# Where the four links of a weight scale's chain stand in a step of a fused attention and MLP kernel

## The chip, the cores and the metric

The kernel runs on one core of one Trainium2 chip. The metric is the device time of one execution in microseconds. The core has five engines with queues of their own: TensorE (PE; matmuls and, listed apart as PEld, weight loads), VectorE (DVE), ScalarE (ACT), GpSimd (POOL) and SyncE (SP, which here only issues transfers). An engine takes its instructions in the order in which the program lists them, and waits at each for the semaphores that it needs. So where an instruction stands in its engine's list decides what waits behind it. In order of time, three runs of the kernel before took 994.47, 989.99 and 993.67 us, with a median of 993.67.

## The reference

Causal attention over 4 batches of 8 heads, 576 positions and 64 dimensions, with an added bias from the running sum of `max(s, 0)`; then a first MLP, `relu(x w_in)^2 w_out`, and a second, `h cos(h) w_out` with `h = x w_in`, over 2304 tokens, model size 512 and hidden size 2048.

```python
scores = scale * np.matmul(q, k.transpose(0, 1, 3, 2))
cum = np.cumsum(np.maximum(s, 0.0), axis=-1)
bias = -(cum[:, :, :, None] - cum[:, :, None, :])
scores = np.where(causal, -1e9, scores + np.minimum(bias, 0.0))
x = softmax(scores) @ v            # then to (2304, 512)
h = np.maximum(x @ w_in, 0.0);  x = h * h @ w_out      # first MLP
h = x @ w2_in;  out = h * np.cos(h) @ w2_out           # second MLP
```

## The kernel before, in words

Products are made of parts: a weight tile is scaled by a power of two and split into a high half and the rest, and three products (high by high, high by low, low by high) stand for one.

The program's first part is a sequence of calls of `step()` (line 1236). I number them from 1. Call n emits the scores of attention job n - 1 (`emit_qk`), the mask and minimum of the job before (`emit_mask`, L593), the exponential (`emit_exp`, L616), the transposes of the probabilities (`emit_turn`, L629), their copy out of PSUM (L650), the products with V (`emit_pv`, L695), and every fourth call the transposes of an output (`turn`, L757), which ScalarE (`x_high`, L800) and VectorE (`x_low`, L816) read and split. A job is 128 queries of one head; the first sixteen heads have two jobs each, with 128 and 256 keys. From call 22 on a call also takes one or two slots of the first MLP: `g1` (L1078, twelve matmuls into `hps`), whose result ScalarE takes with Relu, square and cast (L1089 to L1091) and VectorE splits (L1097), and `g2` (L1107).

Beside that each call prepares weights of the first MLP, one half row of 512 columns at a time: loaded by SyncE (L207), rescaled by ScalarE (L924), put together from two integer halves by VectorE (L930, L934), then written as the high part by ScalarE (`w_hi`; L946 with a scale, L950 without) and the rest by VectorE (`w_lo`; L964, L969). `room()` and the buffers `st`, `xst` and four spare halves of `wt` say how many can be under way.

The high part of a `w_in` tile needs a scale, a power of two for each pair of tiles, and that has a chain of its own, which also serves two blocks of tokens (from V):

1. `gram()`: eight matmuls of the tiles with themselves (L831) into `xps[:, 384:512]`; the trace of this is the sum of the squares of each row's columns.
2. `gram_sums()`: VectorE multiplies with the identity and adds up along the row (L836).
3. `gram_total()`: a matmul with ones adds over the 128 rows (L845) into `xps[:, 264]`.
4. `gram_scale()`: VectorE takes the exponent (L853), POOL makes scale and inverse (L860, L866), and the pair goes on the list `wrest`, from which the next `w_step` takes it to `w_hi`.

The chain runs ten times: for eight pairs of tiles (pair 0 to 7) and for two blocks of tokens. Its PSUM tile `xps` is also that of the output's transposes (columns 0 to 255) and of V's sums (L459). In the kernel before, link 1 stands near the end of call n, link 2 at the head of call n + 1, link 3 behind the first MLP slot of that call, and link 4 ahead of the mask and of `w_step`, all in the same call. The trace of a pair stands in calls 8, 11, 14, 21, 24, 26, 29 and 32, that of the two blocks in calls 6 and 13. The list `later` holds work that is due at a given call; a call takes at most one entry from it.

Of the kernel before, what the change touches and what calls it, by code (L numbers as in the profile page):

```python
# [36 lines left out]
W_AHEAD = 2.5  # L37
GRAM, GSUM = 384, 264
SPARES = 4


def _weave(*chains):
# [81 lines left out]
V_STRIDE = 11  # L124
V_NEAR = 6
V_TIME = 7
X_AT = (4, 12)


@with_exitstack  # L130
def attention_moe_moe_kernel(
# [290 lines left out]
    def load_v(n):  # L422
        b, h, nch = heads[n][1], heads[n][2], (heads[n][7] + 127) // 128
        if n < EARLY:
            vd[n] = vown[n]
            return
        vb = at.tile([128, 5, 2, D], F16, tag="vb", bufs=4, name="vb")
        nc.sync.dma_start(out=vb[:, 0:nch], in_=v_d[b, h, :, 0:nch])
        vd[n] = vb
# [175 lines left out]
    def emit_exp(i):  # L605
        n, ti, q, r = jobs[i]
        h = heads[n][2]
        j = jd[i]
        x = h % 2
        if _paired(heads[n]):  # L610
            if x == 0:
                return
            r, x = 128, 0
        w, sb = j["w"], j["sb"]
        z = pd[n - h % 2]["z"]
        nc.scalar.activation(  # L616
            out=sb[0:r, 0:w], in_=sb[0:r, 0:w], func=ACTF.Exp, scale=-1.0, bias=j["nb"],
            accum_out=z[0:r, ti, x:x + 1],
        )
        if _paired(heads[n]):  # L620
            nc.scalar.copy(z[0:64, 0, 1:2], z[64:128, 0, 0:1])
# [11 lines left out]
    def p_turn():  # L633
        while turned:
            pt, p = turned.pop(0)
            nc.sync.dma_start_transpose(out=pt, in_=p)
# [147 lines left out]
    def x_high():  # L784
        for k, c, o, m, pt, _ in xcq:
            if k not in xb:
                xb[k] = (
                    m1.tile([128, KD, BT], F16, tag="xh", bufs=2, name="xh"),
                    m1.tile([128, KD, BT], F16, tag="xl", bufs=2, name="xl"),
                )  # L790
        while kept.get("go"):
            k = kept["go"].pop(0)
            for (o, m), cs in kept.pop(k).items():
                c0, c1 = min(cs), max(cs) + 1
                xs = [t[:, c0:c1, o:o + m] for t in (x32, *xb[k])]
                nc.scalar.activation(out=xs[1], in_=xs[0], func=ACTF.Copy, scale=xsc[:, k:k + 1])
                convq.append((k, xs))
        for k, c, o, m, pt, _ in xcq:
            if k in xready:
                nc.scalar.activation(  # L800
                    out=xb[k][0][:, c, o:o + m], in_=pt[:, 0:m], func=ACTF.Copy, scale=xsc[:, k:k + 1]
                )
            else:
                nc.scalar.copy(x32[:, c, o:o + m], pt[:, 0:m])
                kept.setdefault(k, {}).setdefault((o, m), []).append(c)
# [17 lines left out]
    def gram():  # L823

        if not gq or dq:
            return
        key, aps = gq.pop(0)
        out = xps[:, GRAM:GRAM + 128]
        for n, t in enumerate(aps):
            t = t.bitcast(BF16)[:, 1::2]  # L830
            nc.tensor.matmul(out, t, t, start=(n == 0), stop=(n == len(aps) - 1))  # L831
        dq.append(key)

    def gram_sums():
        for key in dq:
            nc.vector.scalar_tensor_tensor(  # L836
                out=gjunk, in0=xps[:, GRAM:GRAM + 128], scalar=1.0, in1=ident, op0=ALU.mult, op1=ALU.mult,
                accum_out=dss[:, key:key + 1],
            )
        oq.extend(dq)  # L840
        dq.clear()

    def gram_total():
        for key in oq:
            nc.tensor.matmul(xps[:, GSUM:GSUM + 1], ones, dss.bitcast(BF16)[:, 2 * key + 1:2 * key + 2])  # L845
        eq.extend(oq)
        oq.clear()

    def gram_scale():

        while eq:
            key = eq.pop(0)
            nc.vector.tensor_scalar(  # L853
                out=gex, in0=xps[:, GSUM:GSUM + 1].bitcast(I32), scalar1=24, scalar2=23, op0=ALU.logical_shift_right,
                op1=ALU.logical_shift_left,
            )
            sc, iv = (wsc1, wiv1) if key < NF // 2 else (xsc, xiv)
            c = key % (NF // 2)
            for t, a, b in ((sc, -1, 205), (iv, 1, 254 - 205)):
                nc.gpsimd.tensor_scalar(  # L860
                    out=t[:, c:c + 1].bitcast(I32), in0=gex, scalar1=a, scalar2=b << 23, op0=ALU.mult, op1=ALU.add
                )
            if sc is xsc:
                xready.add(c)
            else:
                nc.gpsimd.tensor_scalar(  # L866
                    out=hs1[:, 0, c:c + 1], in0=wiv1[:, c:c + 1], scalar1=xiv[:, 0:1], scalar2=1.0, op0=ALU.mult,
                    op1=ALU.mult,
                )
                wrest.extend(pairs.pop(c))  # L870
# [22 lines left out]
    def job(i):  # L893
        return jobs[i] if 0 <= i < NJ else None
# [16 lines left out]
    nw = [2, 0, 0]  # L911
# [27 lines left out]
    def w_hi(j):  # L939
        m, f, a = wq[j]  # L940
        if m == 0 and a == 0:
            t = wp.tile([128, 2, 512], F32, tag=f"w{2 * f}", name="wt")
            wt[0, f, 0] = t[:, 0].bitcast(F16).rearrange("p (a c) -> p a c", a=2)
            if f < SPARES:
                free.append(t[:, 1])
# [273 lines left out]
    def stage(s, i):  # L1219

        while stages[s] <= i and job(stages[s]):
            stages[s] += 1
            yield stages[s] - 1
# [7 lines left out]
    def values(i):  # L1231
        for j in stage(0, i - 2):
            if jobs[j][1] == 0:
                load_v(jobs[j][0])

    def step(moe=0, bits=0, attn=True):

        i = prog[0]
        held = len(xtq)
        prog[0] += attn  # L1240
        if attn:
            for j in stage(1, i - 2):
                emit_exp(j)
        x_high()
        if attn and job(i - 2):
            emit_turn(i - 2)
        if attn:
            heads_ahead(i, (next_, load_ext, 2))
        w_age()
        w_scales()  # L1250
        gram_sums()
        n = moe_slot() if moe else None
        gram_total()
        slow = bool(vq) and any(f is v_wait for f, g in vq[0])
        if slow:
            v_sums()
        if attn:
            heads_ahead(i, (nhigh, prep_high, 2))
        _weave(evacuate())
        y_evict()  # L1260
        if not attn or g2done[0] < 2:
            rests()
        if xcq and xcq[-1][-1] and xcq[-1][0] == 1:
            x_low()
        gram_scale()
        _weave(softmax_tail(i) if attn else None, w_step(bits), None if slow else v_early())
        x_low()
        rests()
        w_lows()
        if attn and job(i - 1) and jobs[i - 1][0] < EARLY:  # L1270
            for j in stage(1, i - 1):
                emit_exp(j)
        act(n)
        if attn:
            heads_ahead(i, (nlow, prep_low, 2))
        if slow:
            _weave(v_early())
        if not (attn and last_block(i)):
            y_store()
        if attn and job(i):  # L1280
            emit_qk(i)
        if attn and last_block(i):
            heads_ahead(i, (nraw, load_raw, 4))
        for _ in range(moe - 1):
            act(moe_slot())
            y_evict()
        w_sums()
        if attn:
            for j in stage(1, i - 1):
                emit_exp(j)  # L1290
        behind = any(job(j) and _paired(heads[jobs[j][0]]) for j in (i - 6, i - 5))
        if attn and not behind:
            values(i)
        turn(held if moe and i > last_job[0] + TURN_FROM else len(xtq))
        if not slow:
            v_sums()
        gram()
        if attn:
            for j in stage(3, i - LAG[0]):
                if j > i - lag(j):  # L1300
                    stages[3] -= 1
                    break
                emit_pv(j)
        if attn and behind:
            values(i)
        p_turn()
        w_ahead()
        if attn:
            heads_ahead(i, (nraw, load_raw, 4))
        v_late()  # L1310
        y_store()
        if later and prog[0] >= later[0][0]:
            later.pop(0)[1]()
# [18 lines left out]
    def w_age():  # L1332
        wsum.extend(wsq)
        wsq.clear()
# [18 lines left out]
    def w_lows():  # L1353
        while wlow:
            w_lo(wlow.pop(0))
# [71 lines left out]
    later.append((4, store_c1))  # L1427
    later.append((X_AT[0], lambda: early_scale(0)))
    later.append((6, lambda: v_own(1)))
    later.append((8, lambda: store_ones(nc.sync, EARLY, len(heads))))  # L1430
    later.append((11, store_c))
    later.append((X_AT[1], lambda: early_scale(1)))
    for n in seg0[EARLY // H:]:
# [280 lines left out]
```

## Time and profile before

| | |
|---|---|
| median of three runs | 993.67 us (989.99 to 994.47) |
| the profiled execution | 994.07 us, of which the span from first to last instruction is 992.2 us |
| mean granted TensorE clock | 0.973 of full speed |
| TensorE busy | 949.5 us, 96% of the span |
| VectorE busy | 724.9 us, 73% |
| ScalarE busy | 674.8 us, 68% |
| POOL busy | 171.9 us, 17% |

Shares over the whole span are means over unlike stages. The four links of the chain all fall in the first 110 us, and there the table has to be read stretch by stretch. In a list of instructions, what stands in brackets is the idle time of the engine just before, and what ended it. Matmuls are pipelined and the ends of their rows are modelled, so neighbouring rows overlap.

### The profile page before, as it was taken

To read this page: it belongs to the slowest core of one execution; us is meant where nothing else is said; L and a number is where in the kernel's file an instruction comes from. 1 tells how busy PE (TensorE), PEld (TensorE's weight loads), DVE (VectorE), ACT (ScalarE), POOL (GpSimd) and SP (SyncE) were. 2 spreads that over 40 slices of the span, in tenths; PEclk is the share of its full clock that TensorE was granted. 3 is DMA by queue.
4 is the path that set the end of the run, shared out by engine and by line. 5 is a ranking of instruction groups with operands and counts; after the bars stand their busy time and mean duration, and the time that the engine had idled before them with its cause. 6 is when DMAs were issued, how large, how long until landed. Compare 5 with 4: busy or idle time off the path is not lost.

```text
span 992.2 us, 20635 instructions
## 1 busy us (share of the span) xinstructions
PE 949.5 (96%) x7340; PEld 699.2 (70%) x7340; DVE 724.9 (73%) x1868; ACT 674.8 (68%) x1599; POOL 171.9 (17%) x279
## 2 busy tenths in 40 slices
PE   6888889999999999999999999999999999999998
PEld 5677778888899988889989987444544454444444
DVE  6758878777887877787898265798779865545555
ACT  6568877778888878778786587667657743334333
POOL 3001101111110111111111022431133340001101
PEclk8579899999999999999999999999999999999999
DMA  8766249865898986568899579210000000001001
GB/s 258 231 223 199 64 117 216 214 169 148 183 185 171 203 194 173 143 149 170 184 215 191 168 265 356 96 43 1 1 1 1 1 1 1 12 32 43 33 10 65
DMA packets 150520, 127.22 MB, mean 128 GB/s; under 512 B 107864, under 2 KB 125600, under 8 KB 150416
## 3 DMA queue, kind: packets, MB, share of 16 engines
q1 hardware_dynamic: 146512, 119.59, 46.8%
q0 software_dynamic: 3904, 6.30, 2.6%
q8 instruction: 58, 0.95, 0.4%
q14 instruction: 46, 0.38, 0.1%
HBM read 85.79 MB, written 15.83 MB: 102 GB/s over the span
## 4 chain that ended last, share of the span: by engine, by line
PE 76%; DVE 8%; ACT 7%; DMA 5%; issue 3%; SPq 1%; DVEq 0%; POOL 0%; ACTq 0%
PE hp L1535 19%; PE o L1590 18%; PE y L1107 15%; PE hps L1078 15%; PE qkp L575 4%; PE pvs L702 3%; DMA rw<-in_w_dram 2%; DMA raw<-in_qk_dram 2%; ACT sb L616 1%; ACT g L1089 1%; DVE k L418 1%; DVE sb L593 1%; ACT g L1090 1%; PE xps L757 1%; DMA early<-in_qk_dram 1%
## 5 line engine op out<-in xcount | busy, mean ns | idle before, releaser
L1107 PE MATMUL y<-gh,wt 128*128 128x256 f32 x1152 | 239.0, 290 | 2.1 <-DVE wt L969 2.1
L1078 PE MATMUL hps<-xh,wt 128*128 128x256 f16 x1152 | 217.0, 276 | 8.8 <-ACT g L1089 8.8
L1107 PEld LDWEIGHTS y<-gh,wt 128*128 128x128 f32 x1152 | 189.3, 191 | 3.8 <-DVE wt L969 2.6
L1078 PEld LDWEIGHTS <-wt 128*128 128x128 f16 x1728 | 161.9, 99 | 35.2 <-issue 13.2
L1535 PE MATMUL hp<-yh,wt 128*128 128x512 f16 (+1 forms) x640 | 185.9, 358 | 0.0
L1590 PE MATMUL o<-wt,gh 128*128 128x512 f16 x576 | 171.3, 379 | 0.1
L1107 PE MATMUL y<-gl,wt 128*128 128x256 f32 x576 | 163.3, 283 | 0.5 <-DVE gl L1097 0.5
L1078 PE MATMUL hps<-xl,wt 128*128 128x256 f16 x576 | 158.9, 276 | 0.0
L1535 PEld LDWEIGHTS <-wt 128*128 128x128 f16 x960 | 91.9, 98 | 93.0
L1547 ACT ACTIVATE a<-hp,hsc 128x512 f32<-128x512 f32 (+1 forms) x80 | 51.5, 643 | 111.6 <-PE hp L1535 109.8
L1089 ACT ACTIVATE g<-hps,hs 128x256 f32<-128x256 f32 x144 | 67.6, 469 | 75.6 <-PE hps L1078 69.3
L1535 PE MATMUL hp<-yl,wt 128*128 128x512 f16 (+1 forms) x320 | 114.4, 358 | 0.0
L1107 PEld LDWEIGHTS y<-gl,wt 128*128 128x128 f32 x576 | 110.2, 191 | 1.4 <-DVE gl L1097 0.9
L1590 PE MATMUL o<-wt,gl 128*128 128x512 f16 x288 | 109.2, 379 | 0.0
L1548 DVE TENSOR_SCALAR kf<-a 128x512 f32<-128x512 f32 (+1 forms) x80 | 36.0, 450 | 93.2 <-ACT a L1547 92.9
L1590 PEld LDWEIGHTS <-gh 128*128 128x128 f16 x576 | 56.3, 98 | 64.6 <-ACT gh L1570 0.6
L400 POOL DMA_DIRECT2D k<-ext_d x80 | 41.8, 522 | 296.3 <-ACT g L1089 37.7
L616 ACT ACTIVATE sb<-sb,nb 128x128 f32<-128x128 f32 (+7 forms) x152 | 87.4, 575 | 5.2 <-DVE nb L593 5.0
L1556 ACT ACTIVATE a<-kf 128x512 f32<-128x512 f32 (+1 forms) x80 | 46.8, 584 | 50.8 <-DVE kf L1549 49.9
L1097 DVE TENSOR_TENSOR gl<-g,gh 128x256 fp32r<-128x256 f32 x144 | 60.4, 419 | 23.7 <-ACT gh L1091 15.6
L593 DVE CUSTOM_DVE_ANT_0 sb<-qkp,mask 128x128 f32<-128x128 f32 (+7 forms) x152 | 69.2, 456 | 4.5 <-PE qkp L560 1.8
L661 DVE SCALAR_TENSOR_TENSOR p<-sb,p 128x384 f16<-128x384 f32 (+3 forms) x120 | 66.4, 553 | 3.7
(160 smaller groups left out, 1676.0 us busy)
## 6 DMA issues: line engine op xcount, KB each, us to landing
rw<-in_w_dram SPq DMA_DIRECT2D x64, 512.0 KB
raw<-in_qk_dram SPq DMA_DIRECT2D x48, 352.0 KB
raw<-in_qk_dram SPq DMA_DIRECT2D x16, 384.0 KB
v_d<-vt SPq DMA_DIRECT2D x16, 320.0 KB
vb<-v_d SPq DMA_DIRECT2D x32, 160.0 KB
vr<-in_v_dram POOLq DMA_DIRECT2D x15, 320.0 KB, 4.6
y_d<-st SPq DMA_DIRECT2D x18, 256.0 KB
yr<-y_d SPq DMA_DIRECT2D x9, 512.0 KB
```

The costliest lines, as they stand in the source:

```text
L400: nc.gpsimd.dma_start(out=hd[n][1][64:68, BT - nq:BT + nl], in_=ext_d[n, :, BT - nq:BT + nl])
L593: nc.vector.tensor_tensor_reduce(out=sb[0:r, c0:c0 + cn], in0=p[0:r, 0:cn], in1=mask[0:r, mo:mo + cn], scale=-0.125, scalar=(3.0e38 if k = ...
L616: nc.scalar.activation(out=sb[0:r, 0:w], in_=sb[0:r, 0:w], func=ACTF.Exp, scale=-1.0, bias=j["nb"], accum_out=z[0:r, ti, x:x + 1],)
L661: nc.vector.scalar_tensor_tensor(out=p[0:r, cw:cw + w], in0=sb[0:r, 0:w], scalar=PSC, in1=p[0:r, 0:w], op0=ALU.mult, op1=ALU.subtract,)
L1078: nc.tensor.matmul(hp, w[:, a, c * 128:(c + 1) * 128], (xh, xl)[e][:, c, :], start=(n == 0), stop=(n == 3 * KD - 1),)
L1089: nc.scalar.activation(out=g, in_=hp, func=ACTF.Relu, scale=hs1[:, k % 2, f // 2:f // 2 + 1])
L1097: nc.vector.tensor_tensor(out=gl, in0=g, in1=gh, op=ALU.subtract)
L1107: nc.tensor.matmul(yps[k][d // 2][:, d % 2, :], w[:, a, d * 128:(d + 1) * 128], (gh, gl)[e], start=(f == 0 and n == 0 and d % 2 == 0), sto ...
L1535: nc.tensor.matmul(hp, w[:, a, c * 128:(c + 1) * 128], (yh, yl)[e][:, c, :], start=(m == 0), stop=(m == 3 * KD - 1),)
L1547: nc.scalar.activation(out=a, in_=hp, func=ACTF.Copy, scale=sm["hsc"][:, j, f:f + 1], bias=0.25)
L1556: nc.scalar.activation(out=a, in_=kf, func=ACTF.Sin, scale=-6.2831850)
L1590: nc.tensor.matmul(ops[j][a], (gh, gl)[e][:, a * 128:(a + 1) * 128], w[:, x, :], start=(first and m == 0), stop=(last and m == 2),)
```

## The change

The chain is spread over more calls. Trace products stand at the end of call n, behind the products with V; the sum stands in call n + 1 behind `w_lows`, the total at the end of call n + 1, the power in call n + 2 behind `w_lows`, and the scaled copies follow in call n + 3. Where a call has an MLP slot and 26 or more half rows have been prepared (`nw[2] >= QUICK_FROM`), sum, total and power keep their old places. `X_AT` is the call from which the first block's chain is due.

```diff
+QUICK_FROM = 26
...
-X_AT = (4, 12)
+X_AT = (5, 12)
...
-        gram_sums()
+        quick = moe and nw[2] >= QUICK_FROM
+        if quick:
+            gram_sums()
         n = moe_slot() if moe else None
-        gram_total()
+        if quick:
+            gram_total()
...
-        gram_scale()
+        if quick:
+            gram_scale()
         _weave(softmax_tail(i) if attn else None, w_step(bits), None if slow else v_early())
         x_low()
         rests()
         w_lows()
+        gram_scale()
+        gram_sums()
...
         if not slow:
             v_sums()
-        gram()
         if attn:
             for j in stage(3, i - LAG[0]):
...
         if attn and behind:
             values(i)
+        gram_total()
+        gram()
         p_turn()
```

Three places in the order of the two programs follow. Lines of the changed program stand one or, behind the new lines, some more below those of the kernel before (L836 is L837 there, L946 is L947).

VectorE in call 9, where the sum of pair 0 (`gjunk`) and the power (`gex`) stand; before:

```order
L836 SCALAR_TENSOR_TENSOR gjunk,dss<-xps,ident 128x128
L853 TENSOR_SCALAR gex<-xps 128x1
L593 ISA sb,nb<-qkp,mask 128x256
L593 ISA nb 128x1
L930 TENSOR_SCALAR st<-st 128x512
L650 COPY pt_311<-qkp 128x128
L934 SCALAR_TENSOR_TENSOR st<-rw,st 128x512
L816 SCALAR_TENSOR_TENSOR xl<-xps,xsc,xh 128x256
L964 SCALAR_TENSOR_TENSOR wt<-st,wsc_93,wt 128x512 x2
```

The same place in the changed program, to the power of pair 0 in call 10:

```order
L594 ISA sb,nb<-qkp,mask 128x256
L594 ISA nb 128x1
L931 TENSOR_SCALAR st<-st 128x512
L651 COPY pt_301<-qkp 128x128
L935 SCALAR_TENSOR_TENSOR st<-rw,st 128x512
L817 SCALAR_TENSOR_TENSOR xl<-xps,xsc,xh 128x256
L837 SCALAR_TENSOR_TENSOR gjunk,dss<-xps,ident 128x128
L594 ISA sb,nb<-qkp,mask 128x128
L594 ISA nb 128x1
L854 TENSOR_SCALAR gex<-xps 128x1
```

The sum has moved from ahead of the mask (`sb`) to behind the split of the output (`xl`), the power into the next call, and the two subtractions of pair 0 (`wt`) have left the call.

ScalarE in call 22, the first with an MLP slot, where the scaled copies of pair 3 (`wt` with `wsc`) stand; before:

```order
L924 ACTIVATE st<-rw 128x512
L946 ACTIVATE wt<-st,wsc_93 128x512
L946 ACTIVATE wt<-wt,wsc_93 128x512
L650 COPY pt_642<-qkp 128x256
L616 ACTIVATE sb,z<-sb,nb 128x128
L1089 ACTIVATE g<-hps,hs_95 128x256
```

The same place in the changed program:

```order
L925 ACTIVATE st<-rw 128x512
L651 COPY pt_632<-qkp 128x256
L617 ACTIVATE sb,z<-sb,nb 128x128
L1090 ACTIVATE g<-hps,hs_95 128x256
L1091 ACTIVATE g<-g 128x256
L1092 CAST gh<-g 128x256
```

The two scaled copies are gone from ahead of the copy of transposed probabilities (`pt`), the exponential (`sb,z`) and the Relu (`g<-hps`); they stand in call 24.

VectorE in call 25, with the sum of pair 4; before:

```order
L836 SCALAR_TENSOR_TENSOR gjunk,dss<-xps,ident 128x128
L853 TENSOR_SCALAR gex<-xps 128x1
L593 ISA sb,nb<-qkp,mask 128x256
L593 ISA nb 128x1
L930 TENSOR_SCALAR wt<-wt 128x512
L650 COPY pt_848<-qkp 128x128
L934 SCALAR_TENSOR_TENSOR wt<-rw,wt 128x512
L816 SCALAR_TENSOR_TENSOR xl<-xps,xsc,xh 128x256
L1097 TENSOR_TENSOR gl<-g,gh 128x256
L969 TENSOR_TENSOR wt<-wt 128x512
L964 SCALAR_TENSOR_TENSOR wt<-xst,wsc_93,wt 128x512 x2
```

The same place in the changed program:

```order
L594 ISA sb,nb<-qkp,mask 128x256
L594 ISA nb 128x1
L931 TENSOR_SCALAR wt<-wt 128x512
L651 COPY pt_838<-qkp 128x128
L935 SCALAR_TENSOR_TENSOR wt<-rw,wt 128x512
L817 SCALAR_TENSOR_TENSOR xl<-xps,xsc,xh 128x256
L1098 TENSOR_TENSOR gl<-g,gh 128x256
L970 TENSOR_TENSOR wt<-xst,wt 128x512
L837 SCALAR_TENSOR_TENSOR gjunk,dss<-xps,ident 128x128
```

The sum now ends the call's work on VectorE, behind one subtraction (`wt<-xst,wt`); the pair's own two subtractions have moved two calls on.

## Rows read from the trace of the kernel before

**Rows 1.** The page, part 2: granted TensorE clock in 40 slices, in tenths.
```profile
PEclk8579899999999999999999999999999999999999
```

**Rows 2.** Stretch, length; busy of PE, PEld, DVE, ACT, POOL (instructions); PEclk, DMA share, GB/s.
```profile
17.38:41.76 24.38, 19.42 (x94) 16.03 (x93) 14.43 (x52) 13.00 (x33) 3.11 (x11) 0.50 0.96 298
41.76:51.02 9.26, 8.90 (x36) 7.41 (x36) 8.44 (x29) 6.92 (x20) 0.00 (x0) 0.50 0.30 94
51.02:60.46 9.44, 6.53 (x33) 4.90 (x32) 4.45 (x14) 3.56 (x11) 1.28 (x3) 0.61 0.82 285
60.46:110.44 49.98, 45.27 (x365) 40.61 (x365) 38.24 (x110) 44.07 (x110) 5.42 (x12) 0.93 0.49 157
110.44:992.20 881.76, 859.76 (x6774) 622.62 (x6773) 647.58 (x1629) 596.60 (x1404) 154.88 (x235) 1.00 0.48 118
```

**Rows 3.** Instructions on tile xps: count, ns min/median/max, first and last start.
```profile
L836 DVE SCALAR_TENSOR_TENSOR gjunk<-xps,ident x10: 275/291/292, 14.1 to 109.8; 128x128 bf16<-128x128 f32 x10
...
L845 PE MATMUL xps<-dss,ones x10: 163/167/211, 14.5 to 110.2; 128*128 128x1 bf16 x10
L853 DVE TENSOR_SCALAR gex<-xps x10: 157/158/159, 14.7 to 110.4; 128x1 int32<-128x1 int32 x10
```

**Rows 4.** What PE waited for, 17.6 to 54.3 us: us in total, times, longest.
```profile
PE qkp L629 <- ACT sb L616: 3.1, 4, 1.1
PE xps L831 <- DMA early<-in_qk_dram: 1.1, 1, 1.1
PE xps L831 <- DVE xl L816: 0.9, 1, 0.9
PE xps L831 <- DVE xst L934: 0.5, 1, 0.5
PE xps L845 <- DVE gjunk L836: 0.3, 1, 0.3
```

**Rows 5.** What ACT waited for, 0 to 60.46 us.
```profile
ACT wt L946 <- POOL wsc L860: 11.3, 4, 5.9
...
ACT st L924 <- DMA rw<-in_w_dram: 2.7, 1, 2.7
```

**Rows 6.** Timeline of DVE in call 9: start, us, instruction, idle before.
```profile
20.32 0.29 DVE L836 SCALAR_TENSOR_TENSOR gjunk<-xps,ident 128x128 bf16<-128x128 f32 x1 [2.88 <-ACT xh L800]
```

**Rows 7.** Timeline of PE in calls 22 and 23.
```profile
57.32 1.17 PE L560 MATMUL qkp<-early 66*128 66x256 f32 x2
60.46 0.27 PE L1078 MATMUL hps<-xh,wt 128*128 128x256 f16 x1 [1.97 <-ACT g L1089]
```

**Rows 8.** Timeline of ACT in call 22.
```profile
58.06 0.72 ACT L946 ACTIVATE wt<-st,wsc 128x512 f16<-128x512 f32 x1 [5.85 <-POOL wsc L860]
58.69 0.71 ACT L946 ACTIVATE wt<-wt,wsc 128x512 f16<-128x512 f32 x1
...
59.95 0.46 ACT L1089 ACTIVATE g<-hps,hs 128x256 f32<-128x256 f32 x1
```

**Rows 9.** What PE waited for, 60.4 to 110.5 us.
```profile
PE qkp L629 <- ACT sb L616: 2.3, 2, 1.9
...
PE xps L845 <- DVE gjunk L836: 1.3, 2, 0.8
PE xps L459 <- DVE xl L816: 0.5, 1, 0.5
PE xps L831 <- DVE xl L816: 0.4, 1, 0.4
```

**Rows 10.** The chain that ended last, 95 to 110 us: start, us, what.
```profile
100.81 2.30 PE hps L1078 x12
...
105.59 1.32 PE hps L1078 x12
```

**Rows 11.** Timeline of PE at the end of call 25.
```profile
76.06 0.16 PE L459 MATMUL xps<-ss,ones 128*128 128x2 bf16 x1 [0.50 <-DVE xl L816]
```

**Rows 12.** Timeline of DVE in call 25.
```profile
76.86 1.40 DVE L964 SCALAR_TENSOR_TENSOR wt<-xst,wsc,wt 128x512 f16<-128x512 f32 x2
```

## The prediction

> **What bounds the kernel now.** I read the shares over the whole span first: TensorE is busy 96% of it, and its granted clock is low only in the first slices of 24.8 us [rows 1]. The code says that the changed chain runs ten times, once for each of eight weight pairs and once for each of two blocks of tokens, and the trace puts all ten power instructions between 14.7 and 110.4 us [rows 3]; from call 36 on, about 120 us, both programs have the same instructions in the same order on every engine. So I cut the first 110 us into stretches [rows 2]. From 17.38 to 41.76 us, from the scores of call 8 to those of call 16 with four chains between, TensorE is busy 19.42 of 24.38 us at a granted clock of 0.50 (1.2 GHz). From 41.76 to 51.02 us, five calls without any chain, it is busy 8.90 of 9.26 us at the same clock. From 51.02 to 60.46 us, where the trace of pair 3 stands, only 6.53 of 9.44 us. From 60.46 to 110.44 us TensorE has 45.27 and ScalarE 44.07 of 49.98 us, so both are near their limit. Behind that TensorE has 859.76 of 881.76 us, so what is won ahead of it should stay won: nothing there starts by a fixed time.
>
> Then who waits for whom. In 17.6 to 54.3 us TensorE waited 3.1 us in four places for the exponentials of L616 [rows 4]. ScalarE was late with these because it stood, in its own queue, behind L946, which waited 11.3 us in four places for the weights' scale [rows 5]. Later the same pair of waits is 2.3 us on TensorE [rows 9].
>
> **The change, part by part.** It adds and removes no instruction. On the five engines it moves these:
>
> *The trace products* (L831, eight matmuls) go behind the call's products with V, and so does *the total* (L845). They cost TensorE the same there: 0.16 us for a total [rows 3]. *The sum* (L836) and *the power* (L853) go on VectorE from the head of a call to behind the subtractions of `w_lows`, the power a call later than before. The scaled copies (L946) thereby come two calls later. For the last pair, at `nw[2]` of 26 or more, sum, total, power and copies keep their old places, so nine chains of ten change. *X_AT* from 4 to 5 costs and gives nothing: the list it feeds gives up one entry a call and has entries for calls 2, 3 and 4 ahead of it, so this one comes in call 5 either way. SyncE's queue is the same in order. On POOL one load (L400) passes ahead of pair 6's three small instructions; nobody waits for these before the next call.
>
> Term 1, calls 8 to 16. VectorE stood 2.88 us ahead of the sum of pair 0, with the mask of the next scores queued behind it [rows 6], and what follows it in the chain ends in the ScalarE wait above. After the change mask, exponentials and transposes go first. TensorE's work stays, so I let the stretch run at the share that the chainless calls show: 19.42 x 9.26 / 8.90 = 20.2 us in place of 24.38, a gain of 4.2 us. VectorE then has 14.43 us to do in 20.2 (71%, against 91% in the chainless calls), ScalarE 13.00, so neither need pace it. Bounds: no gain, if another engine or the transfers pace it, to 5.0 us, all of TensorE's idle time. I take 4.2, next to the waits that bear a name up to 51 us, 3.1 + 1.1 + 0.5 + 0.3 = 5.0 us [rows 4], of which the chainless calls hold 0.3.
>
> Term 2, calls 21 and 22. ScalarE waited 5.85 us for pair 3's scale, because its total stood behind the whole first GEMM slot, and the first Relu (L1089) came at 59.95 us; TensorE waited for it 1.97 us, its scores having ended at 57.32 + 1.17 = 58.49 us [rows 7, 8]. The Relu is now ahead of the scaled copies and can start when the GEMM ends, about 57.3 us; the 1.97 us go. TensorE's wait of 0.9 us ahead of the trace, for L816, is covered by the products with V that now stand first, except 0.1. Gain 2.8 us; bounds 0 and 2.9, the idle time of the stretch.
>
> Term 3, 60.46 to 110.44 us. TensorE's waits there that a changed chain makes: 2.3 for exponentials, 1.3 - 0.8 for sums (the 0.8 is the last pair's, which stays), 0.5 and 0.4 for L816, together 3.7 us [rows 9]. The clock adds to it: behind the longest of these waits it fell to 0.5 and twelve matmuls took 2.30 in place of 1.32 us [rows 10], so the end above is 4.7 us. Against it: the two scaled copies of pair 3, 1.34 us, leave a stretch where ScalarE idled and come into this one, where it has 44.07 us of 49.98. If ScalarE took every one of them from the gain and the waits only moved, the term would be -1.3 us. I take the middle, 1.7 us.
>
> Other covers. The copies come two calls later, but the first GEMM slots use each pair at least a call after its new place (pair 6, the latest, is subtracted at the head of call 32 and used in call 33), and no buffer is short: the same tiles are put together in each call as before. If that cover went, a slot would wait for a copy and a subtraction. The transfers: DMA share is 0.96 in the first stretch but 0.30 in the next, with the same queue order, so the loads had run ahead of their use; ScalarE waited for a weight tile once, 2.7 us, before 17 us [rows 2, 5].
>
> Sum: 4.2 + 2.8 + 1.7 = 8.7 us, from the profiled execution's 994.07 us (span 992.2) to 985.4 us. The median of the runs shown, 993.67, is 0.4 us under that execution; I leave 985.4 as it is.
>
> One rule speaks against the change. The trace and total go to columns 264 and 384 of the same PSUM tile whose first 256 columns take the transposes, and at pair 0 the sum, which reads the one, ended its wait with the ScalarE copy of L800, which reads the other [rows 6]; before the trace of pair 3 TensorE waited 0.9 us until L816 had read its own columns [rows 4]. So the one tile passes from engine to engine as a whole. The Trainium skill, "PSUM — Partial Sum Buffer", section "PSUM bank collisions raise a hardware error", says that PSUM must be guarded by bank and quadrant and not by address; the trace agrees with it in these two waits. By it, each sum and power that is moved behind the subtractions holds TensorE's next entry into that tile for as long; that is the second rival below.
>
> **The rivals.** *Paced elsewhere.* The chain's waits go, and the mask and the subtractions on VectorE, the loads or ScalarE take their place. For it: DMA at 0.96 in the first stretch and VectorE at 91% in the next [rows 2]. Against it: 71% by the sum above. Term 1 then gives about 1, term 2 keeps 1.5, term 3 gives nothing: 994.07 - 2.5 = 991.6 us.
>
> *The bank moves the wait to TensorE.* In call 25 TensorE's entry to the tile at 76.06 us waited 0.50 us for L816, while VectorE went on to subtractions until about 78.2 us [rows 11, 12]. With sum and power behind these, the total and the next transposes wait for them, in order, with everything behind them on TensorE. Of 18 visits (nine sums, nine powers) seven have subtractions ahead of them, eleven in all, at 0.70 us (1.40 for two [rows 12]) 7.7 us; the visits themselves take 9 x 0.29 + 9 x 0.16 = 4.1 us [rows 3]. If TensorE paid all of it, 11.8 us: 994.07 - 8.7 + 11.8 = 997.2 us, slower. It decides from 8.7 / 18 = 0.5 us a visit. Against it: in calls 25 and 27 the pair's own subtractions leave the place, and VectorE no longer stands idle before them (2.88 us at pair 0).
>
> *The clock comes up early.* It was 0.50 from 17.38 to 51.02 us [rows 2], with TensorE at 80 to 96%. The Trainium skill, "TensorE: Matmul & The Clock Gate", section "What's actually happening", has it that the slow clock is the default and that activity releases it; the trace agrees in that the clock was full for most of the stretch from 60.46 us. If the fuller calls raise it in the first stretch, VectorE paces: (14.43 + 8.44) / 0.91 = 25.1 us for 33.64, a gain of 8.5 in place of 4.2, and term 3 reaches 4.7: 994.07 - 8.5 - 2.8 - 4.7 = 978.1 us. Against it: the 96% of the chainless calls did not raise it.
>
> **How the numbers follow.** My forecast has 0.62, with its own range 981 to 989.5 us; paced elsewhere 0.22; the bank 0.08; the clock 0.08. A measurement of this kernel can tell about 0.5%, 5.0 us, from no change. Faster by more than that (under 988.7): nearly all of the forecast and the clock case, 0.67. Within it: the paced case and the rest, 0.25. Slower: 0.08. The range reaches down to 979.0, short of the clock case, and up to 994.0, the paced case with nothing won; what it leaves out has about 0.15.
>
> **What would show it.** Term 1 is right if the eight calls take near 20 us, the four waits of TensorE for L616 shrink under 1.5 us in sum, and L946 no longer waits for the scale; wrong if TensorE waits for L836 or L853 instead. Term 2 is right if the second GEMM slot follows the scores within half a microsecond; term 3 if the stretch to the last power takes about 48 us with no 1.9 us wait in it. If the last power comes 8 to 9 us earlier and the end does not, the gain was given back behind it, and my reading of the last stretch was wrong.

## The result, and the profile after

The changed kernel took 985.76 us (median of nine runs, 982.75 to 988.81) against 993.73 us of the kernel before (nine runs, 989.99 to 997.64): 0.9915 of it, with a 95% interval of 0.9896 to 0.9933, so 8.0 us won. The forecast was 985.4 us. In a second set it took 986.20 us against 993.98, a ratio of 0.9936 (0.9911 to 0.9961).

The profiled execution took 988.11 us (span 986.3). Its granted clock by slices, from the page, answers to [rows 1]:

```profile
PEclk9589899999999999999999999999999999999999
```

The stretches of the changed kernel, cut at the same instructions as [rows 2] (scores of calls 8, 16 and 21, second GEMM slot, last power, end), with the same columns:

```profile
17.34:35.72 18.38, 14.88 (x93) 13.16 (x93) 13.48 (x51) 11.43 (x31) 2.58 (x10) 0.78 0.92 283
35.72:46.55 10.83, 9.18 (x37) 7.32 (x36) 9.38 (x31) 8.13 (x22) 0.65 (x3) 0.50 0.88 281
46.55:52.43 5.88, 5.55 (x31) 4.39 (x31) 3.58 (x11) 2.45 (x9) 0.00 (x0) 0.58 1.02 340
52.43:103.38 50.95, 44.67 (x367) 40.55 (x366) 39.03 (x112) 45.65 (x113) 5.39 (x15) 0.93 0.49 167
103.38:986.30 882.92, 861.34 (x6774) 623.44 (x6773) 647.56 (x1629) 597.00 (x1402) 155.15 (x235) 1.00 0.48 118
```

(The clock of the first stretch, 0.78, is too high; the last section says why.) Against 24.38, 9.26, 9.44 and 49.98 us, the first stretch won 6.0 us, the second lost 1.6, the third won 3.6, and the fourth lost 1.0. The last power stands 7.1 us earlier, as the instructions on tile `xps` show (count, ns min/median/max, first and last start), beside [rows 3]:

```profile
L846 PE MATMUL xps<-dss,ones x10: 163/167/211, 15.9 to 103.1; 128*128 128x1 bf16 x10
L854 DVE TENSOR_SCALAR gex<-xps x10: 149/152/159, 17.8 to 103.4; 128x1 int32<-128x1 int32 x10
```

What ScalarE waited for, 0 to 104 us, answers to [rows 5]. The wait for the scale, 11.3 us in the shorter stretch of before, is down to 0.4:

```profile
ACT pt L651 <- PE qkp L630: 7.8, 9, 1.9
ACT sb L617 <- DVE nb L594: 5.3, 6, 1.6
...
ACT wt L947 <- POOL wsc L861: 0.4, 1, 0.4
```

VectorE had waits of the chain too, which the prediction showed in one row only [rows 6]. In the kernel before, 17.3 to 60.46 us:

```profile
DVE gex L853 <- PE xps L845: 5.5, 4, 3.6
DVE gjunk L836 <- PE xps L831: 3.6, 4, 1.1
DVE gjunk L836 <- ACT xh L800: 2.9, 1, 2.9
```

In the changed kernel, in the same calls (17.3 to 52.43 us), neither `gex` nor `gjunk` is among the waits listed for VectorE. TensorE has new ones. From the scores of call 8 to the last power, the list begins:

```profile
PE xps L758 <- DVE xp L743: 2.0, 1, 2.0
PE xps L460 <- DVE gjunk L837: 2.0, 1, 2.0
PE qkp L630 <- ACT sb L617: 1.6, 3, 1.1
PE xps L758 <- DVE gjunk L837: 1.5, 1, 1.5
PE xps L846 <- DVE gjunk L837: 1.5, 3, 0.7
PE xps L758 <- DVE gex L854: 1.4, 2, 0.9
```

The wait for exponentials (L630) fell from 3.1 + 2.3 us [rows 4, 9] to 1.6. But the sum (`gjunk`) and the power (`gex`), which stand behind VectorE's other work now, hold TensorE for 6.4 us in these rows, and the first row is a wait that the kernel before did not have. The second GEMM slot follows its scores without a wait, where 1.97 us stood in [rows 7], and the Relu [rows 8] starts as its GEMM ends:

```profile
51.70 0.60 PE L561 MATMUL qkp<-early 66*128 66x256 f32 x2
52.43 0.27 PE L1079 MATMUL hps<-xh,wt 128*128 128x256 f16 x1
```

```profile
51.90 0.47 ACT L1090 ACTIVATE g<-hps,hs 128x256 f32<-128x256 f32 x1 [1.53 <-PE hps L1079]
```

### The profile page after: what moved, and what is told of

It is laid out like the page before. It is cut to its first block, busy times and chain, and to the rows that moved or that the text cites. A ratio compares the mean times of both kernels' runs of the same rounds, so it can differ in the third digit from the quotient of the medians.

```text
span 986.3 us, 20637 instructions
## 1 busy us (share of the span) xinstructions
PE 946.0 (96%) x7340; PEld 697.4 (71%) x7340; DVE 724.0 (73%) x1868; ACT 675.4 (68%) x1599; POOL 170.5 (17%) x279
## 4 chain that ended last, share of the span: by engine, by line
PE 78%; DVE 8%; ACT 7%; DMA 3%; issue 3%; POOL 1%; SPq 0%; DVEq 0%; ACTq 0%; POOLq 0%
PE hp L1543 19%; PE o L1598 19%; PE y L1108 16%; PE hps L1079 15%; PE qkp L576 4%; PE pvs L703 3%; DMA raw<-in_qk_dram 1%; ACT sb L617 1%; ACT g L1090 1%; PE xps L758 1%; ACT g L1091 1%; DMA vb<-v_d 1%; DVE wt L965 1%; DVE k L419 1%; DVE st L935 1%
## 5 line engine op out<-in xcount | busy, mean ns | idle before, releaser
L1555 ACT ACTIVATE a<-hp,hsc 128x512 f32<-128x512 f32 (+1 forms) x80 | 51.5, 644 | 111.7 <-PE hp L1543 109.9
```

The source lines that it names most:

```text
L1555: nc.scalar.activation(out=a, in_=hp, func=ACTF.Copy, scale=sm["hsc"][:, j, f:f + 1], bias=0.25)
```

## The experiments

A program's time scatters by some 4 us about its median, a few runs by 5 to 7, so for single steps I go by the stretches of the profiles, cut as above. The changed kernel's two profiles agree within 0.5 us in each of the first four stretches. But five profiles below have one order of work in calls 8 to 16 (changed twice, calls 8 to 16 only, pair 6 in turn twice), and took 17.57 to 18.81 us there. Each ratio goes by the kernel before in the same set of runs, whose medians were 993.73 us (the set of "changed", one group of chains at a time and "pair 6 in turn"), 994.85 ("pair 6 in turn, again", "both" and the last row) and 993.98 (the other four). In the last row the last pair's power stands later in the order too, so its fourth stretch does not compare with the others. Behind the last power the time ranged from 878.86 to 885.81 us over all profiles, in no order that follows the edits: that part holds the scatter.

| kernel | calls 8-16 | 16-21 | 21 to slot 2 | slot 2 to last power | median | ratio (95%) |
|---|---|---|---|---|---|---|
| before | 24.38 | 9.26 | 9.44 | 49.98 | 993.73 | |
| changed | 18.38 | 10.83 | 5.88 | 50.95 | 985.76 | 0.9915 (0.9896 to 0.9933) |
| changed, again | 18.81 | 10.82 | 6.13 | 51.03 | 986.20 | 0.9936 (0.9911 to 0.9961) |
| calls 8 to 16 only | 18.45 | 10.82 | 8.07 | 50.16 | 988.84 | 0.9946 (0.9928 to 0.9964) |
| pair 3 only | 23.45 | 9.23 | 6.14 | 49.75 | 989.20 | 0.9957 (0.9940 to 0.9974) |
| pairs 4 to 6 only | 23.47 | 9.25 | 8.56 | 48.81 | 992.32 | 0.9980 (0.9963 to 0.9997) |
| products only | 23.16 | 9.21 | 7.71 | 49.80 | 992.28 | 0.9983 (0.9969 to 0.9997) |
| copies late only | 20.97 | 10.09 | 7.70 | 53.37 | 993.23 | 1.0000 (0.9983 to 1.0018) |
| pair 6 in turn | 17.57 | 10.82 | 5.62 | 48.60 | 985.48 | 0.9904 (0.9880 to 0.9927) |
| pair 6 in turn, again | 18.22 | 10.82 | 5.65 | 48.60 | 982.93 | 0.9883 (0.9861 to 0.9905) |
| sums ahead | 16.86 | 10.94 | 6.06 | 47.71 | 983.84 | 0.9901 (0.9877 to 0.9925) |
| both | 18.73 | 10.82 | 6.23 | 46.30 | 982.63 | 0.9876 (0.9852 to 0.9900) |
| both, last pair too | 16.99 | 10.94 | 5.99 | 49.03 | 984.85 | 0.9901 (0.9876 to 0.9925) |

**One group of chains at a time.** Three kernels spread the chain in one stretch each; the products stand in their new place in all three.

```diff
-        quick = moe and nw[2] >= QUICK_FROM
+        quick = bool(moe)                                    # calls 8 to 16 only
+        quick = not (moe and nw[2] <= 12)                    # pair 3 only
+        quick = not (moe and 13 <= nw[2] < QUICK_FROM)       # pairs 4 to 6 only
```

Calls 8 to 16 only:

> The chain is spread only in calls without an MLP slot (both blocks of tokens and pairs 0 to 2); pairs 3 to 7 keep the old places of sum, total and power. The trace products stand behind the products with V in every call. Theory (the waits for the scale go, place by place): the scores of call 16 at about 35.7 us as in the changed kernel (41.76 before), those of call 21 at 46.5 (51.02 before), then ScalarE waits 5 to 6 us for pair 3's scale again and the second GEMM slot starts near 56 us (60.46 before); the time is 4 to 5 us under before, ratio 0.9955. Rival (the granted clock, which came up at 20.7 us in the changed kernel, made the gain and not the waits): clock 0.5 throughout calls 8 to 16, call 16 at 39 us or later, ratio above 0.998.

Pair 3 only:

> Only pair 3's chain is spread; all others keep sum, total and power where they were; trace products behind the products with V in every call. Theory: call 16 near 41.8 and call 21 near 51.0 us as before, no ScalarE wait of 5.85 us for pair 3's scale, second GEMM slot near 57 us (60.46 before): 2.8 to 3.6 us won, ratio 0.9967. Rival (moving the trace products alone does much of it): call 16 more than 1 us ahead of before. Second rival (a gain at this place is given back by the calls with slots): second slot near 57 us but the last power near 110 us, ratio 0.999.

Pairs 4 to 6 only:

> Only the chains of pairs 4, 5 and 6 are spread; all others keep sum, total and power where they were; trace products behind the products with V in every call. By the prediction's third term the stretch from the second GEMM slot to the last power takes 48.3 us in place of 49.98. By the trace of the changed kernel it takes about 51 us, because pair 6's copies and subtractions are pulled to the head of call 32 and TensorE waits there about 2 us for the mask and the transposed output: second slot near 60.5, last power near 111.5 us, ratio 1.000 to 1.002. If the loss in the changed kernel came from its earlier start instead (transfers or clock at another moment), the stretch takes 48 to 49 us here.

In the first two kernels the stretch whose own chains were spread took about the changed kernel's length, in the third it did not. The medians won 4.9, 4.5 and 1.4 us, 10.8 together, more than the 8.0 of the whole. In the first, call 16 came at 35.67 and call 21 at 46.49 us, as its theory had it; the second slot (54.56 us) came 1.4 us before what it expected (the products stand in their new place there too). With pair 3 only, call 16 came 1.4 us ahead of before, as its first rival had it; the second slot came at 55.74 us, and the last power at 105.49, so that the gain was not given back. With pairs 4 to 6 only, the fourth stretch took 48.81 us: within the 48 to 49 of the last theory named, by which the changed kernel lost by its earlier start (transfers or clock at another moment), and not the 51 of the pull at call 32. TensorE's wait in call 32 came all the same:

```profile
103.98 0.44 PE L758 MATMUL xps<-ident,xp 128*128 128x128 f32 x2 [2.00 <-DVE xp L743]
```

But the granted clock did not fall behind it, as it did at 99.2 us in the changed kernel.

**The trace products alone.**

```diff
-        gram()
         if attn:
             for j in stage(3, i - LAG[0]):
...
         if attn and behind:
             values(i)
+        gram()
         p_turn()
```

> The kernel before with only the trace products moved behind the products with V; sum, total, power and copies stay. From the two runs that held this edit beside one group of pairs: calls 8 to 16 take 23.5 us (24.38 before), call 21 to the second GEMM slot 8.6 us (9.44), everything else as before; 1.5 to 2 us won, ratio 0.998 to 0.9985. If the three gains of the separate groups add up to more than the whole change only because each holds this edit, it is worth (4.9 + 4.5 + 1.4 - 8.0) / 2 = 1.4 us. Rival (the products cost the same anywhere): calls 8 to 16 within 0.3 us of before, ratio 1.000.

As expected: 1.7 us by the medians, and 1.2 us in calls 8 to 16. (Its third stretch, 7.71 us, was shorter than the 8.6 expected.) The clock has a part in both: it was full from 19.6 to 23.0 us and again from 53.7, in the middle of the first slot. With pair 3 only and pairs 4 to 6 only it was low in all of calls 8 to 16, going by the durations (1.06 us and more for two score products of 66x256, 0.60 at full clock; no record covers these calls), and the products gave 0.9 us there. Counted once instead of three times, the groups give 10.8 - 2 x 1.7 = 7.4 us beside 8.0 and 7.8 for the whole, so the medians add up within their scatter. The last stretch does not: counted in the same way, the groups won 0.9 us there (-0.2, 0.2 and 1.2, less twice 0.2), and the changed kernel lost 1.0. So some loss shows only in the whole.

**The copies alone, late.** This is the mechanism on which the prediction's first term rests: ScalarE behind L946.

```diff
-                wrest.extend(pairs.pop(c))
+                hold.append((prog[0] - 1 + 2 * (nw[2] < 26), pairs.pop(c)))
+                w_release(prog[0] - 1)
...
         gram_scale()
+        w_release(prog[0] - attn)
```

(`w_release(n)` hands on to `wrest` what is held up to call n.)

> The kernel before, all four links in their old places, but the scaled copies and subtractions of a pair are held back two calls (not for the last pair). Theory (VectorE standing at sum and power ahead of the mask is most of the price; the ScalarE wait for the scale stood beside it): ScalarE no longer waits for the scale, yet TensorE's waits for the exponentials stay above 2 us to call 21, call 21 comes 1 to 2 us ahead of before (4.5 in the changed kernel), the second GEMM slot near 58.5 us (52.4 in the changed kernel). Rival (ScalarE behind the scaled copies is the whole price, as the prediction had it): call 21 about 4 us ahead, second slot near 53 us, ratio 0.992.

Neither was right as a whole. TensorE's waits for the exponentials from call 8 to call 21 fell only from 3.1 to 2.4 us, as the theory had it. Call 21 came 2.8 us and the second slot 4.5 us ahead of before, half-way between the two, and then all of it was lost: 1.000. (The clock was full for 3.4 us of calls 8 to 16 here, which it was not before.) What ScalarE waited for in this kernel, 17.1 to 58 us:

```profile
ACT sb L616 <- DVE nb L593: 5.4, 6, 2.5
...
ACT sb L616 <- DVE z L727: 2.7, 1, 2.7
```

No wait for the scale is left, but the first row was 2.6 us in the kernel before (17.3 to 60.46 us): ScalarE now waits for the mask, which stands behind the sum and the power on VectorE. From the second slot on, TensorE's largest waits in this kernel were the following two, and the stretch took 53.37 us:

```profile
PE xps L845 <- DVE gjunk L836: 2.2, 1, 2.2
PE xps L757 <- DVE xp L742: 2.0, 1, 2.0
```

The second of them is also in the changed kernel. There VectorE's timeline in call 32 reads (start, us, instruction, idle before):

```profile
96.42 1.42 DVE L965 SCALAR_TENSOR_TENSOR wt<-wt,wsc 128x512 f16<-128x512 f32 x2 [1.83 <-ACT wt L947]
97.75 0.16 DVE L728 TENSOR_SCALAR z<-z 128x4 f32<-128x4 f32 x1
97.95 0.18 DVE L739 RECIPROCAL z<-z 128x4 f32<-128x4 f32 x1
98.24 0.42 DVE L743 SCALAR_TENSOR_TENSOR xp<-pvs,z 128x256 f32<-128x256 f32 x1
98.58 0.28 DVE L594 CUSTOM_DVE_ANT_0 sb<-qkp,mask 128x128 f32<-128x128 f32 x1
```

and TensorE's:

```profile
96.45 0.27 PE L1079 MATMUL hps<-xh,wt 128*128 128x256 f16 x1
98.72 0.44 PE L758 MATMUL xps<-ident,xp 128*128 128x128 f32 x2 [2.00 <-DVE xp L743]
```

The two subtractions of pair 6 stand first, because the `g2` slot at the head of this call prepares every half row up to its own number (`w_need`), pair 6's among them, which it does not use. VectorE stands 1.83 us for pair 6's scaled copies, which ScalarE reaches at 95.69 us, then subtracts for 1.42; the output's scaling (`xp`) and the mask follow, and TensorE waits for `xp`.

**Pair 6 in its turn.** The slot prepares only what it uses:

```diff
-        w_need(spot[0, f, 1] + 1)
+        w_need(spot[0, f, 1] + 1, f)
...
-        while wrest and wrest[0] < j:
+        while wrest and wrest[0] < j and wq[wrest[0]][1] <= f:
...
-        while wlow and wlow[0] < j:
+        while wlow and wlow[0] < j and wq[wlow[0]][1] <= f:
```

> The changed kernel, except that the slot at the head of call 32 no longer pulls pair 6's copies and subtractions ahead of the mask: they follow in their turn, and are made ready only for the slot that uses them. Theory (this pull is what term 3 lost): no 2 us wait of TensorE for the transposed output near 98.7 us, call 33 at about 100.8 us (103.11), last power near 101 us (103.38), and the time 2 us under the changed kernel, ratio to before 0.9895. Rival (TensorE or ScalarE is full there, and the wait only moves): call 33 within 0.7 us of the changed kernel's, the time the same as its.

> The changed kernel with pair 6 in its turn once more: the last power near 99.8 us again if its lead of 3.6 us there belongs to the order of work (2.3 of it from the stretch with slots). If the lead lasts, the median of both sets lies 2 us under the changed kernel's; if it is given back behind 110 us, the lead at call 33 is 3 us more than the changed kernel's and the end is the same within 1 us.

In the first of the two runs VectorE scales the output at 93.71 us without standing, and the subtractions come 2.76 us behind it:

```profile
93.71 0.42 DVE L743 SCALAR_TENSOR_TENSOR xp<-pvs,z 128x256 f32<-128x256 f32 x1
...
96.47 1.41 DVE L965 SCALAR_TENSOR_TENSOR wt<-wt,wsc 128x512 f16<-128x512 f32 x2
```

TensorE's 2 us wait for `xp` is gone, and the last power came at 99.75 and 100.19 us (near 101 was expected). Ahead of it TensorE now waits 1.30 us for the last pair's sum (the changed kernel has no wait there), so a part of the wait moved:

```profile
99.48 0.16 PE L846 MATMUL xps<-dss,ones 128*128 128x1 bf16 x1 [1.30 <-DVE gjunk L837]
```

The stretch took 48.60 us in both runs in place of 50.95 and 51.03: 2.4 us. Of these, 1.4 are TensorE's own busy time (43.28 us in place of 44.67), with one fall of the clock in place of two. The twelve runs have a median of 983.67 us, the changed kernel's fifteen 985.76; the first set alone had shown no difference. That is 2.1 us, with intervals of the ratios that still overlap.

**Sum and power ahead of the splits.** The prediction's second rival, tested from its other side: the two leave the end of VectorE's queue.

```diff
+        gram_scale()
+        gram_sums()
         x_low()
         rests()
         w_lows()
-        gram_scale()
-        gram_sums()
```

> The changed kernel with power and sum ahead of the output's split and the subtractions instead of behind them, still behind the mask. If the waits of TensorE for sums and powers in the changed kernel (6.4 us in sum to 103 us) cost time, they fall under 3 us and the time is 1 to 3 us under the changed kernel's 985.76. Rival (TensorE would wait there for the split or the mask anyway): the waits change their name, and the time stays within 1 us.

The price is visible in the changed kernel in call 25, at the entry of [rows 11]. VectorE there:

```profile
65.93 0.48 DVE L817 SCALAR_TENSOR_TENSOR xl<-xps,xsc,xh 128x256 f16<-128x256 f32 x1 [1.15 <-ACT xh L801]
66.33 0.42 DVE L1098 TENSOR_TENSOR gl<-g,gh 128x256 fp32r<-128x256 f32 x1
66.66 0.69 DVE L970 TENSOR_TENSOR wt<-xst,wt 128x512 fp32r<-128x512 f32 x1
67.27 0.28 DVE L837 SCALAR_TENSOR_TENSOR gjunk<-xps,ident 128x128 bf16<-128x128 f32 x1
```

and TensorE, whose v sums wait until the sum has read the tile:

```profile
67.62 0.18 PE L460 MATMUL xps<-ss,ones 128*128 128x2 bf16 x1 [1.95 <-DVE gjunk L837]
```

With the sums ahead, this entry waits 1.02 us, for the split (`xl`). The waits for sums and powers fell from 6.4 to 4.2 us, not under 3. The median is 983.84 us, about 2 us under the changed kernel's, which the intervals do not tell from it; the stretches show more, 47.71 in place of 50.95 us, and 16.86 in place of 18.38. In sum, though, TensorE's listed waits from call 8 to the last power did not fall (11.9 us, against 11.6): some went, others came, as the 1.02 us here. Of the 3.2 us won from the second slot on, 2.7 are TensorE's own busy time (42.01 us in place of 44.67), at a granted clock of 1.00 in place of 0.93:

```profile
50.98:98.69 47.71, 42.01 (x366) 38.34 (x366) 38.74 (x112) 44.62 (x112) 6.76 (x15) 1.00 0.54 184
```

So most of the gain came through the clock, and not all of that is the edit's: the wait for `xp` is still 2.00 us here (at 94.61), and no fall followed it.

**Both.**

> The changed kernel with both edits: pair 6 prepared in its turn, and sum and power ahead of the output's split. If the two losses of the stretch with slots are separate (2.3 us for pair 6, 3.3 us for the sums, by the last power), the last power comes near 96.5 us (103.4 in the changed kernel, 98.69 with the sums ahead alone), call 33 about 13.5 us ahead of before, and the median is 981 to 983 us. If they are one loss (VectorE behind in call 32), the last power stays near 98.5 us and the median near 984.

The last power came at 100.01 us, since call 8 and the stretch to call 16 were later here (18.73 us); but the stretch with slots took 46.30 us, 4.65 less than in the changed kernel. So the two losses are separate: 2.4 by the one edit, 3.2 by the other, most of their sum by both. TensorE's idle time in the stretch, which mostly leaves the falls of the clock out, says the same in smaller numbers: 6.28 us in the changed kernel, 5.32 with pair 6 in its turn, 5.70 with the sums ahead, 4.11 with both. The median, 982.63 us, is 0.9876 of the kernel before, and the lowest of all kernels measured here, though its interval overlaps those of the two single edits.

**The last pair too.** The run with both edits and `QUICK_FROM = 99`.

> As the run beside it with both edits, and the last pair's chain spread like the others, so that all ten are. If the call of the last pair still pays for VectorE standing at its sum and power, 0.5 to 1.5 us more are won by call 36 and the median lies at 981 to 982 us. Rival (the second GEMM of the next slot is waiting for that pair's copies): TensorE waits for a copy or a subtraction of the last pair, and the time is 1 to 3 us above the run beside it.

The rival showed: TensorE waited 1.74 us at 108.39 for a copy (L951), which the run beside it did not. The time was 984.85 us, 2.2 above; the intervals overlap, so that the cost is likely and not shown.

**The changed kernel again.**

> The changed kernel once more, for the spread of its stretches and to stand beside the others on one chip: calls 8 to 16 in 18.4 us within 0.8, calls 16 to 21 in 10.8, call 21 to the second GEMM slot in 5.9, from there to the last power 51.0 us if the 2 us wait for the transposed output at the end of call 32 belongs to the order of work, 49 or less if it was one execution's; median near 985.8 us. If the run with pair 6 in its turn (985.48) is really faster, this median lies 2 us above it on one chip.

The stretches came back, the 2.0 us wait with them. The median, 986.20 us, is 0.7 above the 985.48 that it was to be set against, not 2; the two were not run on one chip.

## Why the prediction was right, and where it was not

The time and its sign were right: 985.76 where 985.4 was said. The sum was not made of the parts that were named, which came to 7.1 us by the last power and not to 8.7. That the two times lie 0.4 us apart is luck: the interval of the ratio alone reaches 1.8 us to either side.

*Term 1* said 4.2 us for calls 8 to 16. These calls gave 6.0 (5.6 in the second profile), but calls 16 to 21 took back 1.6, which the prediction had left out: pair 2's copies and subtractions stand in call 17 now, and the calls that it calls chainless have them. ScalarE's exponential stands behind these copies, and TensorE waits for it:

```profile
39.49 0.71 ACT L947 ACTIVATE wt<-wt,wsc 128x512 f16<-128x512 f32 x1
40.10 0.49 ACT L617 ACTIVATE sb<-sb,nb 128x256 f32<-128x256 f32 x1
```

```profile
40.74 0.48 PE L630 MATMUL qkp<-ident,sb 128*128 128x128 f32 x1 [1.09 <-ACT sb L617]
```

Net 4.4 and 4.0 us. Its mechanism was half of it. The late copies alone give 3.4 us in these calls and 2.6 net, and with the wait for the scale gone TensorE still waited 2.4 us for the exponentials, so standing behind L946 was not the only reason why ScalarE was late with them. The moved products, of which the prediction said that they cost the same in their new place, give 0.9 to 1.2. What is left, 1.0 to 1.7, I put down to sum and power behind the mask, and to the clock; no run shows it by itself. The reading that VectorE's stand at pair 0 "ends in the ScalarE wait" was too short: VectorE stood 12.0 us for the chain up to the second slot, in its own right. And by its own sign the term was wrong in part: in these calls TensorE waited 2.6 us for sums and powers (L837, L854), in both profiles.

*Term 2* said 2.8, measured 3.6 and 3.3 us. The products moved in call 21 gave 0.9 to 1.7 of it (8.56, 8.07 and 7.71 us in the three runs that change nothing else there), pair 3's chain the rest. The bound of 2.9 us was wrong, since it took TensorE's work as fixed: its busy time fell from 6.53 to 5.55 us. More than half of that is the clock, which rose at 51.5 us, so that the scores ahead of the second slot took 0.60 us in place of 1.17.

*Term 3* is the step that failed: 1.7 us were to be won, 1.0 were lost. The term counted one fall of the clock that was to go; the kernel before had two in this stretch (at 61.7 and 99.3 us), and the changed kernel has two as well. The loss is in TensorE's idle time, 6.28 us in place of 4.71. Two sentences did it. "If that cover went, a slot would wait for a copy and a subtraction" was put aside because pair 6 is subtracted a call before it is used. The slot did not wait, but VectorE did, at the head of a call that I had counted as harmless: 2.4 us in the changed kernel, a fall of the clock included. With pairs 4 to 6 only the same 2.0 us wait came without a fall, and the stretch won 1.2 us. And the bank's rival, at 0.08, was more than half real, if not at its price: TensorE waits for sums and powers in the rows above for 6.4 us, 0.36 us on each of 18 visits, where 0.5 was the point from which it would decide. (Of the 6.4, 1.5 are the total waiting for its own sum.) The rule of the Trainium skill that stood behind it ("PSUM — Partial Sum Buffer", section "PSUM bank collisions raise a hardware error": guard by bank and quadrant, not by address) agrees with the 1.5 us (0.7 in the second profile) that the output's transposes (columns 0 to 255) waited for a sum that reads columns 384 to 511.

*The clock* is behind much of what these waits cost. In the stretch with slots, TensorE's busy time was 44.67 us in the changed kernel, with two falls of the granted clock in it, and 42.19 with both edits and none:

```profile
53.71:100.01 46.30, 42.19 (x367) 38.63 (x366) 38.63 (x112) 44.43 (x112) 6.76 (x15) 1.00 0.54 184
```

That is 1.2 us a fall. The profiles agree on it (without that of the last row, which has more work in the stretch): three without a fall have 42.0 to 42.5 us, five with one 43.1 to 43.9, four with two 44.5 to 45.6. In the changed kernel the falls (at 68.5 and 99.2 us) come right behind the two 2 us waits, at 67.62 and 98.72, so that each cost up to 3.2 us and not 2.0. In all thirteen profiles, between 50 and 110 us, TensorE waited 1.9 us or more at a time 23 times. A fall began during or just behind fifteen of these and did not behind the other eight; one more fall, in the last row's kernel, came behind a wait of 1.74 us, and none without a wait. That is in line with the Trainium skill, "TensorE: Matmul & The Clock Gate", section "What's actually happening", by which the slow clock is the default that activity releases; the eight waits without a fall show that one such wait doesn't settle it. So a part of each difference in this stretch is whether a fall happened to follow.

*Rivals.* "Paced elsewhere" did not come: VectorE was busy 13.48 of 18.38 us. "The clock comes up early" came, for part of calls 8 to 10 (20.7 to 27.6 us), but its 25.1 us to call 21 did not (29.2). It is worth 1.7 to 1.9 us there: the kernels with the sums ahead have one order of work in these calls, and took 16.86 and 16.99 us where the clock came up twice, and 18.73 where it stayed low (by the durations, 1.06 us for two products of 66x256, as no record covers them), TensorE being busy 17.32 us of these. An estimate from these rows: with as much added, the changed kernel's 18.38 us would be some 20.2 at the low clock, which is the length that term 1 had worked out; the rest of the 6.0 us would be the clock's.

*Given back behind the last power?* The lead there was 7.1 and 7.0 us in the two profiles, and the medians are 8.0 and 7.8 apart: nothing is lost behind it beyond the scatter. That one profile ended 6.0 us earlier only is such scatter.

Open: how the 1.0 to 1.7 us that is left of term 1 is shared between mask and clock, and what decides whether the clock falls behind a wait.

## What to carry to other kernels

When a chain of small steps is spread so that one engine no longer waits, list everything that the chain's late end passes: the calls that take its work now, the queues that a "needed by" rule pulls it to the head of, and the other users of its buffer. Test the wait that looks largest alone: here, without the moves on VectorE, it bought 4.5 us and gave them all back. Price a wait of TensorE with the slow clock that may follow it.

## What the runs showed of the hardware

The clock of a slice is not a measurement ahead of the first change that was recorded. In the run with pair 3 only, the first record of the granted clock is at 55.3 us, and its stretch from call 8 to call 16 reads 1.00:

```profile
16.91:40.36 23.45, 19.04 (x93) 15.90 (x93) 15.49 (x55) 13.04 (x33) 3.10 (x11) 1.00 0.97 303
```

But the same matmuls (count, busy us, mean ns) took 680 ns there and 390 ns later at full clock (the kernel before's took 634 to 776 ns at a recorded 0.50):

```profile
L561 PE MATMUL qkp<-early 66*128 66x256 f32 x6 | 3.5, 680 | 0.0
```

```profile
L561 PE MATMUL qkp<-early 66*128 66x256 f32 x8 | 2.5, 390 | 0.0
```

So the clock was at 1.2 GHz. The 0.78 of the changed kernel's first stretch counts what lies ahead of its first record, at 20.7 us, as full, too. Durations of one instruction form tell the clock where the row can't.
